# Order of head scores and softmax steps around the start and the end of a decode layer

## The chip, the cores and the metric

One core of a Trainium2 chip runs the kernel. The metric is the time of one execution on the device, in microseconds (us). Times come from repeated runs and from one profiled execution.

## The reference

One token (a row x of 640 values) goes through two layers, each an attention block over a cached window and a small mixer block. The caches K and V, the weights and the order are the same in both layers.

```python
W = 4096                                  # the last 4096 of 32768 cached positions
def A(x):                                 # 32 heads of 192
    q = (x @ wq) by head
    s = einsum("hd,hkd->hk", q, k_cache[:, -W:]) * 192 ** -0.5
    p = softmax(s)
    o = einsum("hk,hkd->hd", p, v_cache[:, -W:])
    return o.reshape(6144) @ wo
def B(x):                                 # one position: the shifted path adds nothing
    x1 = x + 0
    return x1 + gelu(ln(x1) @ w3) @ w4    # 640 -> 1536 -> 640
x = x + A(ln(x)); x = x + B(ln(x))
x = x + A(ln(x)); x = x + B(ln(x))
```

All inputs are bf16. A head's window of K, or of V, is 4096 x 192 values, 1.57 MB. Both layers read nearly all of K and V from memory: 217 MB in all.

## The kernel before, in words

**Loads and cells.** SP issues all loads, in one fixed order (`stream`). K, V and wo go into 11 cells of on-chip memory of 1.57 MB each. `take` hands out the cell that was given back first in program order, and `give` returns one; a load waits on SP until the last use of its cell is over, and everything behind it in the stream waits with it. The wq weights stay resident. The two mixer weights take a cell each at the end of the first layer and keep it.

**Scores.** A head's K is transposed by DVE in four quarters (line 308), which frees the K cell. PE multiplies each quarter with the block form of q (line 358, 48 matmuls a head, 12 a quarter); the result goes to `ST_ps`. In the code `T(h, half)` does two quarters of the transpose and `S(h, half, ...)` the scores of two quarters.

**Kept heads.** In layer 1 (`layer == 0` in the code) the transposed K of heads 0 to 6 (`NKEEP = 7`) stays in seven cells. Layer 2 scores these heads without loading or transposing K again; the cell of a kept head is given back after its second half of scores (`give(("T", h))`). So at the start of layer 2, two cells are taken by mixer weights, seven by kept heads, and two are left for loads. The stream begins layer 2 with V of heads 0, 1, 2, K of head 7, V of head 3 (half of it; the other half waits in PSUM and is copied back by DVE behind the P*V of head 2, line 434), wo of group 0, then K8, V4, K9, V5, K10, V6, K11, V7.

**Groups.** Heads go in eight groups of four: in layer 1 from the last group to the first, in layer 2 from the first to the last. While group g's softmax and P*V run, the scores of group g + 1 are made. The steps of a softmax (`softmax_steps`) are part_max (DVE, line 369), turn_max (PE, line 375), full_max (DVE, lines 380 and 382), spread_max (PE, line 388, then ACT's copy and four exponentials, line 394), swap (PE, line 403, ACT, line 406, PE, line 408) and recip (DVE). The steps of a group's q projection (`qproj_steps`) are project (PE, line 325, 30 matmuls), spread (DVE, line 332), repeat (PE, line 339) and block (DVE, line 344). P*V of a head is `pv` (PE, line 445, 32 matmuls), followed by DVE's transpose into `o_sb` (line 449); `o_fold` is one small product on PE and a scaling on ACT (lines 457 and 458). `out_proj` (line 468) multiplies a group's output with its part of wo. Small products share two PSUM buffers (`psm`).

**The order is written by hand.** Each engine runs its instructions in the order of the program. Before the loop, group 0 is scored, with the first half of its q projection ahead of head 0 and the second half, and `softmax_scale` (1/std of the input; two products on PE and two steps on ACT), ahead of the second head. In the loop, the steps of the softmax are spread between the first two heads of the next group, the other two are scored behind the first two P*V. For the next to last group (`hurry`) both remaining heads are scored behind the second P*V, and the softmax of the last group follows at once: four steps there, the rest behind the third P*V. In layer 2's first pass heads 4 and 5 are scored ahead of the swap, head 6 behind the first P*V, head 7 behind the second.

Of the kernel before, what the change touches and what calls it, by code (L numbers as in the profile page):

```python
# [33 lines left out]
def kernel(  # L34
# [15 lines left out]
    _, _, D = A_x.shape  # L50
    _, H, Sk, Dh = A_k_cache.shape
# [9 lines left out]
    QH = 4  # L61
# [10 lines left out]
    NKEEP, NCELL = 7, 11  # L72
# [240 lines left out]
    def qproj_steps(c, xc, part=None):  # L313

        held = {}
        n = QT if part is None else QT // 2
        t0 = c * QT + (part or 0) * n

        def project():
            need("wq", 0, ND - 1)  # L320
            qT_ps = psm.tile([P, n], F32, tag="psm")
            for tl in range(n):
                t = t0 + tl
                for kc in range(ND):
                    nc.tensor.matmul(  # L325
                        qT_ps[:, tl:tl + 1], lhsT=wq_sb[:, kc, t * P:(t + 1) * P], rhs=xc[:, kc:kc + 1],
                        start=(kc == 0), stop=(kc == ND - 1))
            held["q"] = qT_ps

        def spread():  # L330
            Xq = sm.tile([P, n, 4], BF16, name="Xq")
            nc.vector.tensor_tensor(  # L332
                out=Xq[:], in0=held["q"][:, :].unsqueeze(2).broadcast_to([P, n, 4]),
                in1=maskq[:, :].unsqueeze(1).broadcast_to([P, n, 4]), op=ALU.mult)
            held["x"] = Xq

        def repeat():
            Qrep_ps = psm.tile([P, 4 * n], F32, tag="psm")
            nc.tensor.matmul(Qrep_ps[:], lhsT=Lb[:], rhs=held["x"][:].rearrange("p t b -> p (t b)"),  # L339
                             start=True, stop=True)  # L340
            held["r"] = Qrep_ps

        def block():
            nc.vector.tensor_tensor(
                out=Qblk[:, 4 * t0:4 * (t0 + n), :],
                in0=held["r"][:, :].unsqueeze(2).broadcast_to([P, 4 * n, NM]),
                in1=blkm[:, :].unsqueeze(1).broadcast_to([P, 4 * n, NM]), op=ALU.mult)

        return project, spread, repeat, block
# [125 lines left out]
    def attention(layer, x_cur, rs_cur, x_new, rs_new):  # L475
        groups = GROUPS[layer]
        xc, _, total = ln_center(x_cur, rs_cur)
        y = [x_cur]
        Th = {}
        last_plain = [h for g in groups for h in g if h >= NKEEP][-1]  # L480

        sc = sm.tile([P, 1], F32, name="sc")

        def softmax_scale():
            rstd = power(total(), 1.0, eps1, "rstd")
            nc.vector.tensor_scalar(out=sc[:], in0=rstd[:], scalar1=scale, scalar2=None, op0=ALU.mult)

        def T(h, half):
            for q in (2 * half, 2 * half + 1):
                if (h, q) not in Th:  # L490
                    Th[h, q] = transpose_quart(layer, h, q)

        def S(h, half, ST_ps, hq):
            for q in (2 * half, 2 * half + 1):
                scores_quart(h, Th.pop((h, q)), q, ST_ps, hq)
            if half == 1 and layer == 1 and h < NKEEP:
                give(("T", h))
            if half == 1 and layer == 0 and h == last_plain:
                give(("area", layer))
                area[0] = None  # L500

        def q_now(gi, part=None):
            for step in qproj_steps(groups[gi][0] // QH, xc, part):
                step()

        def add_y(y_ps, last):
            if last:
                nc.vector.scalar_tensor_tensor(out=x_new[:], in0=y_ps[:], scalar=1.0, in1=y[0][:],
                                               op0=ALU.mult, op1=ALU.add, accum_out=rs_new[:, 0:1])
                return  # L510
            y_new = sm.tile([P, ND], F32, name="y_acc")
            nc.vector.tensor_add(y_new[:], y[0][:], y_ps[:])  # L512
            y[0] = y_new

        q_now(0, 0)
        ST = psS.tile([P, 4, NGK, NM], F32, name="ST_ps")
        for hq, h in enumerate(groups[0]):
            if hq == 1:
                q_now(0, 1)
                softmax_scale()  # L520
            for half in range(2):
                if layer == 0:
                    T(h, half)
                else:
                    Th.update({(h, q): transpose_quart(layer, h, q) for q in (2 * half, 2 * half + 1)})
                S(h, half, ST, hq)
        pending = None
        early = None
        for gi, cur in enumerate(groups):
            nxt = list(enumerate(groups[gi + 1])) if gi + 1 < len(groups) else []  # L530
            ST_n = None
            if nxt:
                part_max, turn_max, full_max, spread_max, swap, recip = softmax_steps(len(cur), ST, sc)
                ST_n = psS.tile([P, 4, NGK, NM], F32, name="ST_ps")
                if gi == 0:
                    q_now(1)
                h0 = nxt[0][1]
                T(h0, 0)
                part_max()
                T(h0, 1)  # L540
                S(h0, 0, ST_n, 0)
                turn_max()
                full_max()
                S(h0, 1, ST_n, 0)
                spread_max()
                h1 = nxt[1][1]
                q = None
                if gi + 2 < len(groups):
                    q = qproj_steps(groups[gi + 2][0] // QH, xc)
                if layer == 1 and gi == 0:  # L550

                    for half in range(2):
                        T(h1, half)
                        S(h1, half, ST_n, 1)
                    nxt.pop(1)
                    PT = swap()
                    rl = recip()
                    for step in q:
                        step()
                else:  # L560
                    if q:
                        q[0]()
                    if pending is not None:
                        y_ps = out_proj(layer, *pending)
                    T(h1, 0)
                    if q:
                        q[1]()
                        q[2]()
                    if pending is not None:
                        add_y(y_ps, False)  # L570
                        pending = None
                    PT = swap()
                    T(h1, 1)
                    if q:
                        q[3]()
                    rl = recip()
                nxt.pop(0)
            else:
                if layer == 0:
                    add_y(out_proj(layer, *pending), False)  # L580
                PT, rl = early
            oT = sm.tile([P, NA], BF16, name="oT")
            hurry = gi + 2 == len(groups)
            final = gi + 1 == len(groups)
            fold = None
            for hq, h in enumerate(cur):
                o_sb = pv(layer, h, hq, PT, fold)
                if final:
                    fold = None
                    if hq < QH - 2:  # L590
                        o_fold(h, o_sb, oT, rl)
                    else:
                        def fold(h=h, o_sb=o_sb):
                            o_fold(h, o_sb, oT, rl)

                    continue
                for _ in range(2 if hurry and hq == 1 else 1):
                    if nxt:
                        q2, h2 = nxt.pop(0)
                        for half in range(2):  # L600
                            T(h2, half)
                            S(h2, half, ST_n, q2)
                if hurry and hq == 1:
                    steps = softmax_steps(len(cur), ST_n, sc)
                    steps[0]()
                o_fold(h, o_sb, oT, rl)
                if hurry and hq == 1:
                    for step in steps[1:4]:
                        step()
                if hurry and hq == 2:  # L610
                    early = steps[4](), steps[5]()
            if final:
                if layer == 1:
                    add_y(out_proj(layer, *pending), False)
                fold()
            pending = (cur[0] // QH, oT)
            ST = ST_n
        add_y(out_proj(layer, *pending), True)
# [92 lines left out]
```

## Time and profile before

| | |
|---|---|
| median of 5 runs | 543.34 us (542.81 to 543.76) |
| the profiled execution | 544.75 us, span of the profile 542.9 us |
| PE busy with matmuls | 283.7 us (52%) |
| DVE busy | 257.5 us (47%) |
| ACT busy | 54.6 us (10%) |
| read from memory | 217.06 MB, 400 GB/s over the span |
| granted TensorE clock | 1.00 |

In the profile, busy times are sums over an engine's instructions; a line of waits names who waited for whom; a timeline has start, length, engine, line and form of merged instructions, and in brackets the idle time ahead of them with what ended it ("issue": nothing that the profile shows). Windows give busy times in a stretch of the span, with the mean busy share of the 16 DMA engines and the rate. All times on these views are from the start of the span. The first layer's attention ends near 289 us, its mixer near 296 us, where layer 2 begins.

### The profile page before, as it was taken

To read this page: it belongs to the slowest core of one execution; us is meant where nothing else is said; L and a number is where in the kernel's file an instruction comes from. 1 tells how busy PE (TensorE), PEld (TensorE's weight loads), DVE (VectorE), ACT (ScalarE), POOL (GpSimd) and SP (SyncE) were. 2 spreads that over 40 slices of the span, in tenths; PEclk is the share of its full clock that TensorE was granted. 3 is DMA by queue.
4 is the path that set the end of the run, shared out by engine and by line. 5 is a ranking of instruction groups with operands and counts; after the bars stand their busy time and mean duration, and the time that the engine had idled before them with its cause. 6 is when DMAs were issued, how large, how long until landed. Compare 5 with 4: busy or idle time off the path is not lost.

```text
span 542.9 us, 14848 instructions
## 1 busy us (share of the span) xinstructions
PE 283.7 (52%) x6820; PEld 229.5 (42%) x6820; DVE 257.5 (47%) x494; ACT 54.6 (10%) x249; POOL 2.0 (0%) x11
## 2 busy tenths in 40 slices
PE   0156546365364545545635777656454554636645
PEld 0045435254353434434415755545343443524434
DVE  2187536455554636537212137655463653555511
ACT  1001010010100101010201011010010101001101
POOL 1000000000000000000000000000000000000000
DMA  8999999999999999999999899999999999999980
GB/s 353 426 424 422 421 423 422 422 422 420 424 419 422 425 422 420 425 425 416 370 409 384 310 356 420 423 424 417 426 419 422 421 421 424 421 423 422 423 356 13
DMA packets 23633, 218.00 MB, mean 402 GB/s; under 512 B 2452, under 2 KB 3988, under 8 KB 8084
## 3 DMA queue, kind: packets, MB, share of 16 engines
q1 hardware_dynamic: 23572, 217.07, 96.3%
q8 instruction: 53, 0.87, 0.6%
q14 instruction: 8, 0.07, 0.0%
HBM read 217.06 MB, written 0.00 MB: 400 GB/s over the span
## 4 chain that ended last, share of the span: by engine, by line
DMA 74%; PE 13%; DVE 9%; issue 2%; ACT 1%; SPq 0%; ACTq 0%; DVEq 0%
DMA cell<-in_A_k_cache_dram 54%; DMA cell<-in_A_v_cache_dram 15%; DVE cell L308 7%; PE O_ps L445 4%; PE ST_ps L358 3%; DMA cell<-in_A_wo_dram 3%; DMA wq_sb<-in_A_wq_dram 3%; PE l_ps L408 1%; PE y_ps L468 1%; PE qT_ps L325 1%; PE y_ps L660 1%; PE hT_ps L628 1%; PE PT_ps L403 1%; PE nb_ps L388 0%; ACT PT L406 0%
## 5 line engine op out<-in xcount | busy, mean ns | idle before, releaser
L308 DVE STREAM_TRANSPOSE cell<-cell 128x768 uint32<-128x768 uint32 x228 | 204.4, 946 | 91.9 <-DMA cell<-in_A_k_cache_dram 91.9
L358 PE MATMUL ST_ps<-Qblk,cell 128*128 128x4 bf16 x3072 | 113.8, 168 | 155.4 <-DVE cell L308 153.9
L358 PEld LDWEIGHTS <-cell 128*128 128x128 bf16 x3072 | 97.7, 105 | 187.4 <-DVE cell L308 180.8
L445 PE MATMUL O_ps<-cell,PT 128*1 128x192 bf16 x2048 | 98.3, 359 | 17.1 <-DMA cell<-in_A_v_cache_dram 16.2
L449 DVE STREAM_TRANSPOSE o_sb<-O_ps 128x192 f32<-128x192 f32 x64 | 24.5, 382 | 119.9 <-PE O_ps L445 119.9
L445 PEld LDWEIGHTS <-PT 128*1 128x1 bf16 x2048 | 68.2, 115 | 23.8 <-issue 12.3
L458 ACT ACTIVATE oT<-oT_ps,rl 32x6 bf16<-32x6 f32 x64 | 16.5, 257 | 284.2 <-PE oT_ps L457 284.2
L394 ACT ACTIVATE Pr<-ST_ps,nb_sb,sc 128x32 bf16<-128x32 f32 x64 | 25.1, 488 | 0.5
L325 PE MATMUL qT_ps<-xc,wq_sb 128*128 128x1 bf16 x480 | 16.3, 166 | 15.8 <-DMA wq_sb<-in_A_wq_dram 12.6
L457 PE MATMUL oT_ps<-o_sb,Lq 128*32 128x6 f32 x128 | 17.0, 205 | 12.2 <-DVE o_sb L449 12.1
L325 PEld LDWEIGHTS <-wq_sb 128*128 128x128 bf16 x480 | 15.3, 105 | 16.7 <-DMA wq_sb<-in_A_wq_dram 13.3
L457 PEld LDWEIGHTS oT_ps<-o_sb,Lq 128*32 128x32 f32 x128 | 12.0, 142 | 21.2 <-issue 14.1
L339 PE MATMUL Qrep_ps<-Xq,Lb 128*128 128x24 bf16 (+1 forms) x18 | 3.2, 179 | 28.6 <-DVE Xq L332 28.6
L468 PE MATMUL y_ps<-oT,cell 128*128 128x1 bf16 x480 | 15.3, 166 | 2.9 <-DMA cell<-in_A_wo_dram 1.9
L403 PEld LDWEIGHTS <-Eq 128*32 128x32 bf16 x256 | 4.0, 106 | 29.8 <-DVE y_acc L512 27.4
L468 PEld LDWEIGHTS <-cell 128*128 128x128 bf16 x480 | 14.4, 104 | 3.4 <-DMA cell<-in_A_wo_dram 2.6
L332 DVE TENSOR_TENSOR Xq<-qT_ps,maskq 128x24 bf16<-128x24 f32 (+1 forms) x18 | 2.8, 156 | 26.0 <-PE qT_ps L325 26.0
L390 ACT COPY nb_sb<-nb_ps 128x4 f32<-128x4 f32 x16 | 2.6, 162 | 120.6 <-PE nb_ps L388 120.6
L394 ACT ACTIVATION_READ_ACCUMULATOR Pr<-ST_ps,nb_sb,sc 128x1 f32 x64 | 14.4, 224 | 0.0
L408 PE MATMUL l_ps<-lpart,ones 128*128 128x4 f32 x32 | 9.4, 364 | 5.7 <-ACT PT L406 5.3
L408 PEld LDWEIGHTS l_ps<-lpart,ones 128*128 128x128 f32 x32 | 8.0, 311 | 7.4 <-ACT PT L406 6.7
L388 PE MATMUL nb_ps<-dg,ones 4*128 4x4 f32 x32 | 8.9, 346 | 2.8 <-DVE dg L382 1.7
(85 smaller groups left out, 107.1 us busy)
## 6 DMA issues: line engine op xcount, KB each, us to landing
cell<-in_A_v_cache_dram SPq DMA_DIRECT2D x59, 1536.0 KB, 24.1
cell<-in_A_k_cache_dram SPq DMA_DIRECT2D x57, 1536.0 KB, 26.0
cell<-in_A_wo_dram SPq DMA_DIRECT2D x14, 960.0 KB, 21.6
wq_sb<-in_A_wq_dram SPq DMA_DIRECT2D x5, 1536.0 KB, 12.4
cell<-in_A_v_cache_dram SPq DMA_DIRECT2D x9, 768.0 KB, 19.3
cell<-in_A_wo_dram SPq DMA_DIRECT2D x4, 480.0 KB, 16.0
cell<-in_B_w_dram SPq DMA_DIRECT2D x1, 1536.0 KB, 13.0
cell<-in_B_w_dram SPq DMA_DIRECT2D x1, 1440.0 KB, 14.2
```

The costliest lines, as they stand in the source:

```text
L308: nc.vector.transpose(Tu, Ku[:, :, q * NY:(q + 1) * NY])
L325: nc.tensor.matmul(qT_ps[:, tl:tl + 1], lhsT=wq_sb[:, kc, t * P:(t + 1) * P], rhs=xc[:, kc:kc + 1], start=(kc == 0), stop=(kc == ND - 1))
L358: nc.tensor.matmul(ST_ps[:, hq, q * ng + g, :], lhsT=T4[:, g, f, :, t], rhs=Qblk[:, h * NCOL + 2 * f + t, :], start=(n == 0), stop=(n == N ...
L388: nc.tensor.matmul(nb_ps[:], lhsT=ones[0:n, :], rhs=held["dg"][0:n, :], start=True, stop=True)
L394: nc.scalar.activation(out=Pr[:, hq].rearrange("p m g -> p g m"), in_=ST_ps[:, hq], func=ACTF.Exp, bias=nb_sb[:, hq:hq + 1], scale=sc[:, 0 ...
L403: nc.tensor.matmul(PT_ps[32 * m:32 * (m + 1), :, j, :], lhsT=Eq[:, j, :], rhs=held["Pr"][:, :, m, :], start=True, stop=True)
L408: nc.tensor.matmul(l_ps[:], lhsT=ones[:], rhs=held["l"][:], start=True, stop=True)
L445: nc.tensor.matmul(O_ps[r:r + 1, :], lhsT=PT[:, hq, i:i + 1], rhs=V[:, i * Dh:(i + 1) * Dh], start=(i < 4), stop=(i >= NB - 4))
L449: nc.vector.transpose(o_sb[:], O_ps[:].rearrange("p (a c) -> p c a", c=NA))
L457: nc.tensor.matmul(oT_ps[r, :], lhsT=Lq[:], rhs=o_sb[:, :, 0], start=True, stop=True)
L458: nc.scalar.activation(oT[r, :], oT_ps[r, :], ACTF.Copy, scale=rl[r, 0:1])
L468: nc.tensor.matmul(y_ps[:, n:n + 1], lhsT=wo_t[:, k * D + n * P:k * D + (n + 1) * P], rhs=oT[:, k:k + 1], start=(i == 0 if split else k == 0),
```

## The change

Three orders change; the instructions stay the same.

1. Before the loop, the products of both halves of group 0's q projection come first; the second half's repeat and block come within head 0's scores; `softmax_scale` comes behind the second head. In layer 2, group 1's q projection moves from ahead of the loop into group 0's heads: two steps ahead of the third head, two ahead of the fourth.
2. In layer 2's first pass the kept heads of group 1 (4, 5, 6) are scored in a row with the first steps of the softmax between them. Group 2's projection, the swap and recip follow. Head 7 then comes behind the first P*V.
3. In the next to last group, the last head's second half of scores moves behind the third P*V, with part_max and turn_max; full_max follows the fold; spread_max, swap and recip move behind the fourth P*V.

```diff
-        q_now(0, 0)
+        qa, qb = (qproj_steps(groups[0][0] // QH, xc, part) for part in (0, 1))
+        qa[0]()
+        qb[0]()
+        for step in qa[1:]:
+            step()
+        qb[1]()
         ST = psS.tile([P, 4, NGK, NM], F32, name="ST_ps")
+        q1 = iter(qproj_steps(groups[1][0] // QH, xc))
         for hq, h in enumerate(groups[0]):
-            if hq == 1:
-                q_now(0, 1)
-                softmax_scale()
+            if layer == 1 and hq >= 2:
+                next(q1)()
+                next(q1)()
             for half in range(2):
...
                 S(h, half, ST, hq)
+                if (hq, half) == (0, 0):
+                    qb[2]()
+                    qb[3]()
+            if hq == 1:
+                softmax_scale()
...
                 if layer == 1 and gi == 0:
-                    for half in range(2):
-                        T(h1, half)
-                        S(h1, half, ST_n, 1)
-                    nxt.pop(1)
+                    keep = [hh for hh in nxt if hh[1] < NKEEP]
+                    del nxt[:len(keep)]
+                    q = qproj_steps(groups[2][0] // QH, xc)
+                    part_max()
+                    for i, (q2, h2) in enumerate(keep):
+                        for half in range(2):
+                            T(h2, half)
+                            S(h2, half, ST_n, q2)
+                        if i == 0:
+                            turn_max()
+                            full_max()
+                        if i == 1:
+                            spread_max()
+                    q[0]()
                     PT = swap()
+                    q[1]()
                     rl = recip()
-                    for step in q:
-                        step()
+                    q[2]()
+                    q[3]()
                 else:
+                    if gi == 0:
+                        for step in q1:
+                            step()
...
-                for _ in range(2 if hurry and hq == 1 else 1):
-                    if nxt:
-                        q2, h2 = nxt.pop(0)
-                        for half in range(2):
-                            T(h2, half)
-                            S(h2, half, ST_n, q2)
                 if hurry and hq == 1:
+                    (q2, h2), (q3, h3) = nxt
+                    for half in range(2):
+                        T(h2, half)
+                        S(h2, half, ST_n, q2)
+                    T(h3, 0)
+                    S(h3, 0, ST_n, q3)
+                    T(h3, 1)
+                elif hurry and hq == 2:
+                    S(h3, 1, ST_n, q3)
                     steps = softmax_steps(len(cur), ST_n, sc)
                     steps[0]()
+                    steps[1]()
+                elif nxt and not (hurry and hq == 3):
+                    q2, h2 = nxt.pop(0)
+                    for half in range(2):
+                        T(h2, half)
+                        S(h2, half, ST_n, q2)
                 o_fold(h, o_sb, oT, rl)
-                if hurry and hq == 1:
-                    for step in steps[1:4]:
-                        step()
                 if hurry and hq == 2:
+                    steps[2]()
+                if hurry and hq == 3:
+                    steps[3]()
                     early = steps[4](), steps[5]()
```

More of the change, by code (lines that the diff above doesn't have):

```diff
@@ L500, in S @@
                 area[0] = None
-        def q_now(gi, part=None):
-            for step in qproj_steps(groups[gi][0] // QH, xc, part):
-                step()
         def add_y(y_ps, last):
@@ L534, in attention @@
                 ST_n = psS.tile([P, 4, NGK, NM], F32, name="ST_ps")
[L535 to L549, printed above, removed]
-                if layer == 1 and gi == 0:
-                    for half in range(2):
-                        T(h1, half)
-                        S(h1, half, ST_n, 1)
-                    nxt.pop(1)
+                if layer == 1 and gi == 0:
+                    keep = [hh for hh in nxt if hh[1] < NKEEP]
[12 more added lines that the diff above has]
+                    q[0]()
                     PT = swap()
+                    q[1]()
                     rl = recip()
-                    for step in q:
-                        step()
-                else:
+                    q[2]()
+                    q[3]()
+                else:
+                    if gi == 0:
+                        for step in q1:
+                            step()
+                    h0 = nxt[0][1]
+                    T(h0, 0)
+                    part_max()
+                    T(h0, 1)
+                    S(h0, 0, ST_n, 0)
+                    turn_max()
+                    full_max()
+                    S(h0, 1, ST_n, 0)
+                    spread_max()
+                    h1 = nxt[1][1]
+                    q = None
+                    if gi + 2 < len(groups):
+                        q = qproj_steps(groups[gi + 2][0] // QH, xc)
                     if q:
@@ L576, in attention @@
                     rl = recip()
-                nxt.pop(0)
+                    nxt.pop(0)
             else:
@@ L596, in attention @@
                     continue
-                for _ in range(2 if hurry and hq == 1 else 1):
-                    if nxt:
-                        q2, h2 = nxt.pop(0)
-                        for half in range(2):
-                            T(h2, half)
-                            S(h2, half, ST_n, q2)
-                if hurry and hq == 1:
+                if hurry and hq == 1:
+                    (q2, h2), (q3, h3) = nxt
[7 more added lines that the diff above has]
+                    S(h3, 1, ST_n, q3)
                     steps = softmax_steps(len(cur), ST_n, sc)
                     steps[0]()
+                    steps[1]()
[4 more added lines that the diff above has]
+                        S(h2, half, ST_n, q2)
                 o_fold(h, o_sb, oT, rl)
-                if hurry and hq == 1:
-                    for step in steps[1:4]:
-                        step()
                 if hurry and hq == 2:
+                    steps[2]()
+                if hurry and hq == 3:
+                    steps[3]()
                     early = steps[4](), steps[5]()
```

## The prediction

> **What bounds the kernel now.** I read the chain of waits first, then the rate by slices, then stretches of the boundary between the layers, then the queues of SP and PE there. From the page:
>
> ```profile
> DMA 74%; PE 13%; DVE 9%; issue 2%; ACT 1%; SPq 0%; ACTq 0%; DVEq 0%
> GB/s 353 426 424 422 421 423 422 422 422 420 424 419 422 425 422 420 425 425 416 370 409 384 310 356 420 423 424 417 426 419 422 421 421 424 421 423 422 423 356 13
> ```
>
> The loads bound the kernel: 422 GB/s nearly throughout, while PE is 52% busy and DVE 47%. An instruction moved elsewhere is worth nothing. What can be won is in slices 19 to 23 (258 to 326 us) and in the tail after the last load. The same stretch in windows (us, busy time of PE, PEld, DVE, ACT, POOL, clock, DMA share, GB/s):
>
> ```profile
> 297.00:302.00 5.00, 3.92 (x114) 3.61 (x114) 1.10 (x7) 0.77 (x4) 0.00 (x0) 1.00 0.54 173
> 302.00:310.50 8.50, 5.43 (x187) 5.18 (x185) 0.78 (x5) 0.00 (x0) 0.00 (x0) 1.00 0.99 413
> 310.50:322.00 11.50, 8.82 (x232) 7.41 (x228) 2.59 (x10) 2.26 (x11) 0.00 (x0) 1.00 0.85 316
> 322.00:326.00 4.00, 2.54 (x69) 2.28 (x73) 2.84 (x4) 0.26 (x1) 0.00 (x0) 1.00 0.98 382
> 360.00:500.00 140.00, 74.49 (x1816) 60.90 (x1816) 72.18 (x128) 14.36 (x67) 0.00 (x0) 1.00 1.01 422
> ```
>
> Against 422 GB/s the first window loses 5 x (422 - 173) / 422 = 2.95 us, the third 11.5 x 106 / 422 = 2.89, the fourth 4 x 40 / 422 = 0.38. Why: SP's timeline (start, length, queue and line of the load).
>
> ```profile
> 286.50 13.86 SPq L129 DMA_DIRECT2D cell<-in_A_v_cache_dram  x3
> 302.63 0.33 SPq L117 DMA_DIRECT2D cell<-in_A_k_cache_dram  x1
> 305.19 0.33 SPq L129 DMA_DIRECT2D cell<-in_A_v_cache_dram  x1
> 311.01 0.33 SPq L142 DMA_DIRECT2D cell<-in_A_wo_dram  x1
> 313.09 0.33 SPq L117 DMA_DIRECT2D cell<-in_A_k_cache_dram  x1
> 317.50 0.33 SPq L129 DMA_DIRECT2D cell<-in_A_v_cache_dram  x1
> 318.86 0.42 SPq L117 DMA_DIRECT2D cell<-in_A_k_cache_dram  x1
> ```
>
> By the order of the stream these are V0 to V2 (V2 at 300.0, the row's end), K7, the half of V3, wo0, K8, V4, K9. Each waits for a cell. Data flow about 2.0 us after an issue: V2 at 300.0, the rate is back at 302.0. A whole K or V (1.57 MB) takes 3.73 us at 422, wo0 2.33, the half 1.86. PE in the same stretch:
>
> ```profile
> 297.32 0.54 PE L325 MATMUL qT_ps<-xc,wq_sb 128*128 128x1 bf16 x15 [0.26 <-DVE xc L263]
> 298.58 1.42 PE L358 MATMUL ST_ps<-Qblk,cell 128*128 128x4 bf16 x48 [0.30 <-DVE Qblk L344]
> 301.18 3.98 PE L358 MATMUL ST_ps<-Qblk,cell 128*128 128x4 bf16 x144
> 305.02 0.83 PE L325 MATMUL qT_ps<-xc,wq_sb 128*128 128x1 bf16 x26
> 308.30 0.25 PE L325 MATMUL qT_ps<-xc,wq_sb 128*128 128x1 bf16 x4 [2.45 <-issue]
> 311.62 1.44 PE L358 MATMUL ST_ps<-Qblk,cell 128*128 128x4 bf16 x48
> 317.39 1.44 PE L358 MATMUL ST_ps<-Qblk,cell 128*128 128x4 bf16 x48
> 320.32 0.65 PE L445 MATMUL O_ps<-cell,PT 128*1 128x192 bf16 x12 [0.47 <-issue]
> ```
>
> Heads 0 to 3 are scored by 300.0, 302.5, 303.8 and 305.2, head 4 by 311.0, head 5 by 313.1; head 6 only by 318.8, behind the first P*V. SP's times follow one for one: wo0 has head 4's cell, K8 head 5's, V4 the cell of V0 (P*V ended 317.4), K9 head 6's. PE itself pauses 2.45 us with nothing to wait for, at "issue". A code load of 16 KB begins at 305.7 as it pauses (53 such packets in the instruction queue); 256 instructions are 128 matmuls, 3.4 us here. Counting PE's instructions in the trace in blocks of 256 back from this pause, the time from entering one block to having the next was 6.0 us (302.3 to 308.3) and 5.6 (314.8 to 320.3, the last row's pause).
>
> **The change part by part.** I work on the clock of this execution: 544.75 us with a span of 542.9, 1.41 above the median of 543.34. The saving is subtracted from the median.
>
> *Start of layer 2, V2.* The second projection comes first: 15 more matmuls on PE (15 x 0.031 = 0.47), of which the 0.26 spent waiting for Xq is cover. The repeat starts 0.16 later; the second repeat inside head 0 costs 0.03. Head 0's cell comes free at 300.2, not 300.0. V2 and everything behind it: +0.2.
>
> *Heads 1 to 3.* Head 1 follows at once, but its last matmuls lie in the next code block, which was entered at 302.28 before and can hardly be there sooner: its load began 299.6 and ended 300.7, and 1.5 us more passed at the other pause. So head 1 ends about 302.2 (K7 no later than before). Then 0.5 of softmax_scale, 0.9 of group 1's projection, head 2, and 43 matmuls of head 3, to 306.1. There the count of instructions is that of the old pause. With 6.0 us from 302.1 PE waits until 308.1 and head 3 ends 308.3, 3.1 later than before. It frees V3's half: its data come at 310.3, where K7 ends at 309.8 or so. New gap: 0.5.
>
> *Heads 4 to 6 in a row.* The projection is gone from here. Head 4 by 309.6 (wo0, 1.4 sooner), turn_max, head 5 by 311.0 (K8, 2.1 sooner), 0.5 for the spread of the maxima, then head 6, whose middle lies in the next code block (there at 308.1 + 6.0 = 314.1): it ends at 314.8. V4 now takes head 6's cell: issued 314.8 against 317.50, data at 316.8. The transfers by then: V3's half ends 312.2, wo0 314.5, K8 318.2. All three gaps close, and V4 runs without one.
>
> *P*V of head 0, then head 7.* Projection 0.8, swap 0.3, copy 0.3, l 0.5, P*V 1.4: ends 318.3. K9 gets this cell: data at 320.3, wanted at 321.9, slack 1.6. Head 7 now comes ahead of P*V of head 1: its four transposes (3.52 us) run from 318.7 to 322.3 on DVE, behind nothing but o_sb; V5 takes K7's cell: data at 324.3, wanted at 325.6, slack 1.3. P*V of head 1, the fold and V3's restore stand behind it on PE and DVE, but K10, V6 and K11 have over 3 us each. The first softmax runs beside the scoring: its exponentials end near 313.4 (0.2 and 1.6 after the maxima are spread at 311.5), the swap starts at 315.6.
>
> *Sum.* Recovered 2.89 + 0.38 = 3.27; given back 0.2 + 0.5. That is 2.6 us. It lasts, since from 326 on the queue is ahead and stays so (422).
>
> *Code loading from both sides.* No row shows it in the new order. Not below 5.6 us: head 3 is 0.4 sooner and the gap nearly gone, gain 3.0. The longest such step in the trace is 7.6 (288.4 to 296.0): head 3 ends 309.9, the gap before V3's half is 2.1, V4's 0.1; gain 0.9. I take 6.0, the row in this very stage. The Trainium skill ("Runtime: NRT & Kernel Launch", Instruction fetch mechanics) holds instruction loading to be mostly hidden by the pace of the sequencer; the 2.45 us row says otherwise here, and by the rule alone head 3 would end near 306.3 and the sum be 3.1.
>
> *Start of layer 1.* The same steps, but PE waits 3.8 us for the first K's transposes there, and the loads are at 422. Nothing.
>
> *The last softmax, both layers.* The work is the same; it moves behind the third P*V, its end behind the fourth. DVE's transposes that free K cells keep their places, and no load waits longer: P*V of the third head no longer stands behind half a head's scores, a turn and a spread (262.7 to about 260.2), so V1's and V2's cells come sooner. In layer 1 the next group's first P*V needs the new softmax at about 269.1 against 268.7, and the second waited 1.47 us for V. In layer 2, V27 is there at 512.8, so P*V of head 28 starts near 518.4 instead of 516.57; the waits for loads behind it are 1.49, 0.85, 1.08, 1.01 and 1.55 us. Cost 0; without that cover, 1.9. The tail after the last wo is untouched.
>
> **The rivals.** *Code loading sets the pace.* For it: two pauses in 15 us already. Each block 1.6 us later leaves 0.9: 542.4. *The lost rate is not on the transfer path that ends last.* The 16 engines drift apart by several us; whichever is behind idles less in a gap, so the mean overstates. Against it, the last share of V3's half landed at 311.6 and that of V4 at 326.3: 14.7 us for 9.8 us of bytes (wo0, K8, V4). A gain of some 0.6: 542.7. *Slower: the first P*V starves the queue.* K9 hangs on P*V of head 0 and V5 on head 7, now queued before the second P*V. Beyond 1.3 us of lateness each costs one for one; the gain is gone at 3.9. Two more pauses of 2.45 beyond those counted make 4.9, three 7.4: 543.34 + 7.4 - 3.9 = 546.8. Against it, blocks are 6 us apart and PE waits on DVE there anyway.
>
> **How the numbers follow.** Forecast 543.34 - 2.6 = 540.7, chance 0.68, own range 539.9 (nearly all recovered, restarts cheaper) to 541.6. Code loading 0.13, drift 0.10, starving 0.09. What a measurement can tell is about 0.2%, 1.1 us: faster takes the forecast and two thirds of code loading, 0.77; drift and the rest 0.14; slower 0.09. A range of 539.6 to 542.6 leaves out the starving, half the drift and the lower fringe, under 0.2.
>
> **What would show it.** Right: wo0, K8 and V4 issue near 309.6, 311.0 and 314.8 with x2 at the same time, no second and third gap, V3's half later than 307, an "issue" pause inside head 3's scores. Wrong: V4 issued after 317, a gap at K9 or V5, or PE late for the last wo.

## The result and the profile after

The changed kernel takes 542.19 us (median of 20 runs, 541.49 to 542.96), the kernel before 543.53 (39 runs, 542.18 to 545.12). The ratio is 0.9973, 95% interval 0.9967 to 0.998: 1.3 to 1.5 us faster, where 2.6 were forecast. The profiled execution took 542.02 us with a span of 540.2; that of before took 544.75 with 542.9. The two profiles differ by 2.7 us, and half of that is not in the medians.

The chain of waits and the rate by slices of the changed kernel:

```profile
GB/s 352 428 423 422 418 425 424 422 423 419 423 421 425 422 422 421 422 424 422 409 402 376 297 394 422 421 421 423 425 419 422 422 420 424 421 422 423 422 371 26
DMA 72%; PE 15%; DVE 10%; issue 1%; ACT 1%; SPq 0%; DVEq 0%; ACTq 0%
```

The loads bound it as before; slices 19 to 23 (counted from 0) are still the only dent ahead of the tail. The windows of that stretch (us, busy time of PE, PEld, DVE, ACT, POOL, clock, DMA share, GB/s):

```profile
297.00:302.00 5.00, 4.11 (x131) 3.92 (x132) 0.90 (x6) 0.30 (x2) 0.00 (x0) 1.00 0.42 124
302.00:310.50 8.50, 6.51 (x227) 6.37 (x226) 1.44 (x6) 0.46 (x2) 0.00 (x0) 1.00 0.99 394
310.50:322.00 11.50, 8.25 (x212) 7.08 (x213) 4.59 (x10) 2.26 (x11) 0.00 (x0) 1.00 0.97 386
322.00:326.00 4.00, 2.65 (x54) 1.54 (x43) 1.78 (x4) 0.51 (x2) 0.00 (x0) 1.00 1.02 428
```

The third window went from 316 to 386 GB/s and the fourth from 382 to 428, but the second fell from 413 to 394 and the first from 173 to 124. SP's queue says when each load was issued, in the order V0 to V2, K7, V3's half, wo0, K8, V4, K9:

```profile
286.85 13.60 SPq L129 DMA_DIRECT2D cell<-in_A_v_cache_dram  x3
301.88 0.33 SPq L117 DMA_DIRECT2D cell<-in_A_k_cache_dram  x1
307.82 0.33 SPq L129 DMA_DIRECT2D cell<-in_A_v_cache_dram  x1
309.10 0.33 SPq L142 DMA_DIRECT2D cell<-in_A_wo_dram  x1
310.59 0.80 SPq L117 DMA_DIRECT2D cell<-in_A_k_cache_dram  x1
313.13 0.33 SPq L129 DMA_DIRECT2D cell<-in_A_v_cache_dram  x1
316.62 0.33 SPq L117 DMA_DIRECT2D cell<-in_A_k_cache_dram  x1
```

wo0 came 1.9 us sooner than before, K8 2.5 and V4 4.4; V3's half came 2.6 later, V2 at 300.1 as before. The forecast had 308.3, 309.6, 311.0 and 314.8 for the four loads from V3's half to V4; they came 0.4 to 1.7 sooner. PE shows the reason for V3's half:

```profile
297.37 0.94 PE L325 MATMUL qT_ps<-xc,wq_sb 128*128 128x1 bf16 x30 [0.26 <-DVE xc L263]
299.31 1.98 PE L358 MATMUL ST_ps<-Qblk,cell 128*128 128x4 bf16 x69
301.62 0.22 PE L358 MATMUL ST_ps<-Qblk,cell 128*128 128x4 bf16 x3 [0.34 <-issue]
304.24 1.31 PE L358 MATMUL ST_ps<-Qblk,cell 128*128 128x4 bf16 x44
307.55 1.53 PE L358 MATMUL ST_ps<-Qblk,cell 128*128 128x4 bf16 x52 [1.99 <-issue]
312.32 0.78 PE L358 MATMUL ST_ps<-Qblk,cell 128*128 128x4 bf16 x23 [0.48 <-issue]
```

The three blocks of code end where they were counted to end: in the last matmuls of head 1 (a pause of 0.34), in head 3 (1.99) and in head 6 (0.48). From 301.6, where PE enters a block, to 307.55, where it has the next, are 5.9 us. The block after that was there sooner, at 312.32 or 4.8 us later, and so was V4, which waits for head 6. The moved softmax at the end of layer 2, P*V of head 28, the first three matmuls of head 29's (the other 29 follow at 517.64) and the second half of head 30's:

```profile
515.58 1.45 PE L445 MATMUL O_ps<-cell,PT 128*1 128x192 bf16 x32
517.57 0.33 PE L445 MATMUL O_ps<-cell,PT 128*1 128x192 bf16 x3
521.34 0.81 PE L445 MATMUL O_ps<-cell,PT 128*1 128x192 bf16 x16 [0.83 <-DMA cell<-in_A_v_cache_dram]
```

The first of them starts at 515.58, the 518.4 of the forecast less the 2.7 by which the whole end is earlier, and the waits for V return with the last row (0.83 us). Whether any of it reaches the end is asked of e3 below.

### The profile page after: what moved, and what is told of

Same layout as the page of the kernel before. It is cut to its first block, busy times and chain, and to the rows that moved or that the text cites. A ratio compares the mean times of both kernels' runs of the same rounds, so it can differ in the third digit from the quotient of the medians.

```text
span 540.2 us, 14848 instructions
## 1 busy us (share of the span) xinstructions
PE 282.0 (52%) x6820; PEld 229.2 (42%) x6820; DVE 257.6 (48%) x494; ACT 54.6 (10%) x249; POOL 2.0 (0%) x11
## 4 chain that ended last, share of the span: by engine, by line
DMA 72%; PE 15%; DVE 10%; issue 1%; ACT 1%; SPq 0%; DVEq 0%; ACTq 0%
DMA cell<-in_A_k_cache_dram 57%; DMA cell<-in_A_v_cache_dram 10%; DVE cell L308 8%; PE O_ps L445 5%; PE ST_ps L358 3%; DMA cell<-in_A_wo_dram 3%; DMA wq_sb<-in_A_wq_dram 3%; PE l_ps L408 1%; PE y_ps L468 1%; PE y_ps L688 1%; PE hT_ps L656 1%; PE qT_ps L325 1%; PE PT_ps L403 1%; DVE o_sb L449 0%; PE nb_ps L388 0%
```

## The experiments

The theory: the change gains what the loads V3's half, wo0, K8 and V4 gain by being issued sooner, and the rest of the forecast was lost because V3's half came too late, into a queue that had run dry. The rivals: the last softmax costs what is missing; the first profile of before was a bad execution; or the small loads are slow in themselves. Each ratio is to the kernel before, timed on the same chip.

**The parts of the change, one at a time.** e1 has only the first part of the diff (projections and `softmax_scale`), e2 only the row of kept heads, e3 only the last softmax (lines shortened and run together):

```diff
 e1: +        qa[0]()                # and the rest of part 1
     +            if layer == 1 and hq >= 2: next(q1)(); next(q1)()
 e2: +                    for i, (q2, h2) in enumerate(keep): ...   # q_now(1) stays ahead of it
 e3: +                elif hurry and hq == 2: S(h3, 1, ST_n, q3); ...
```

> Only the first part: both projections of group 0 ahead, softmax_scale behind the second head, group 1's projection inside group 0's heads; the kept heads and the last softmax as before. Theory (gaps): head 3 ends near 308 as in the changed kernel, head 4 near 309.2 without a projection ahead of it, head 5 near 310.6, and P*V of head 0, which frees V4's cell, near 316 instead of 317.5; the second gap closes and most of the third. Nearly the whole gain of the full change, 1.0 to 1.5 us in the medians. Rival (the last softmax eats half): more than the full change gains, 2.4 to 2.8 us.

Measured: 541.96 us against 543.59, ratio 0.9973 (0.9962 to 0.9984): as much as the full change gains. The queue of SP in it, V3's half, wo0, K8 and V4:

```profile
308.19 0.33 SPq L129 DMA_DIRECT2D cell<-in_A_v_cache_dram  x1
309.69 0.33 SPq L142 DMA_DIRECT2D cell<-in_A_wo_dram  x1
311.77 0.33 SPq L117 DMA_DIRECT2D cell<-in_A_k_cache_dram  x1
316.18 0.33 SPq L129 DMA_DIRECT2D cell<-in_A_v_cache_dram  x1
```

K8 and V4 come 1.2 and 3.1 us later than in the full change, and it does not show in the time. With wo0 and K8 still being moved, V4 at 316.2 is not late: the rate from 318 to 322 is 436 GB/s. From 302 to 326 e1 runs at 388 GB/s, the full change at 396; the difference is worth 0.5 us, which these medians can't tell. The forecast gave the third gap to the row of heads; the first part alone closes nearly all of it (379 GB/s from 310.5 to 322, against 316 before and 386 in the full change).

> Only the row of kept heads 4, 5, 6 with group 2's projection behind it; group 1's projection stays ahead of the row, so head 4 still ends near 311 and wo0 is no sooner: the second gap stays, the third (V4, now on head 6's cell near 314.5) goes. Theory (gaps): 0.4 to 1.0 us faster in the medians. Rival (the last softmax eats half): 1.2 to 1.6.

Measured: 542.81 us, ratio 0.9989 (0.9979 to 1.0). About 0.6 us, at the edge of what can be told. V4 came at 314.2, as expected of the row, and wo0 at 310.2, 0.4 to 0.8 us sooner than in the two profiles of before; from 302 to 326 the rate was 381 GB/s. So the row alone raises the rate too (356 and 361 before), but what e1 and e2 gain in rate does not add up in the full change (396).

> Only the move of the last softmax behind the third and fourth P*V of the group before, in both layers. Theory (gaps): the wait is covered, within 0.3 us of before. Rival (the last softmax eats half): 1.0 to 1.4 us slower, with P*V of the last group's heads late for their loads.

Measured: 543.72 us, ratio 0.9998 (0.999 to 1.0006). The last softmax neither costs nor gains more than about half a microsecond; that rival falls.

**The kernel before again (e4).**

> The kernel before, unchanged: a second profiled execution of it. Theory (gaps, the first profiled execution being 1.2 us above the median of all runs): the loss between 302 and 326 us is smaller than the 3.4 us of the first profile, near 2. Rival (the last softmax eats half): the same 3.4 us and a span near 542.9 again.

Measured: 543.75 us over 11 runs, the profiled execution 543.93, span 542.2. Its windows from 310.5 to 326:

```profile
310.50:322.00 11.50, 8.37 (x215) 6.99 (x213) 2.35 (x9) 2.25 (x11) 0.00 (x0) 1.00 0.89 306
322.00:326.00 4.00, 2.72 (x73) 2.46 (x77) 2.67 (x4) 0.26 (x1) 0.00 (x0) 1.00 0.97 400
```

From 302 to 326 the rate was 356 GB/s, 361 in the first profile: a loss of 3.5 to 3.8 us, no smaller. So the first profile was not unlucky there, against my expectation. It differs at the start: PE paused 0.69 us ("issue") at the end of the mixer, where its code packet began at 293.6; here the packet began at 292.5, there was no pause, and V2 was issued at 299.3 instead of 300.0. The forecast used that step only as a bound on a block's length (288.4 to 296.0). Between the profiles at the medians (543.93 and 542.02) lie 1.9 us, not 2.7.

**The new gap at V3's half (e5, e6).** In layer 2 the working cell of DVE's transposes is taken in program order ahead of V3's half, so it gets head 2's cell and V3 head 3's, although it is wanted only near 317. One line in `transpose_quart` turns this round; in e6 it also hands wo0, K8 and V4 a cell one head sooner:

```diff
             if area[0] is None:
+                if layer == 1:
+                    need("v", 1, VKEEP)          # e5;   VKEEP + 1 in e6
                 area[0] = take(("area", layer))
```

> The changed kernel, with the working cell of layer 2's transposes taken behind V3's half in program order: V3's half gets head 2's cell (free near 304.2) and the working cell is head 3's (308). Nothing else moves. Theory (the new gap is an empty queue: V3's half is issued as the queue runs dry, and loads issued one by one into a dry queue reach full rate only after about 3.5 us): V3's half issues near 304.3, the stretch from 309 to 313.5 goes from about 285 GB/s to 380 or more, 0.6 to 1.2 us faster than the changed kernel. Rival (these small transfers are slow in themselves): the stretch stays near 300 GB/s and the time as the changed kernel's.

Measured: 541.49 us, ratio 0.9964 (0.995 to 0.9977), against 541.99 and 0.9974 for the changed kernel timed together with it (e8): 0.5 us, just under the 0.6 expected. V3's half was issued at 304.35 and the stretch from 309 to 313.5 rose to 357 GB/s, less than expected:

```profile
309.00:313.50 4.50, 3.47 (x103) 3.29 (x100) 0.56 (x2) 1.74 (x9) 0.00 (x0) 1.00 1.00 357
```

wo0 came no sooner (309.6), head 6 now paused 1.03 us for code, and V4 came at 314.2, so from 302 to 326 the rate was 393 GB/s and had not risen. The profiled execution, 541.81 us, was the slowest of the seven.

> As the one before, but the working cell is taken behind V4: V3's half, wo0, K8 and V4 each get the cell of one head earlier (heads 2, 3, 4, 5), the working cell is head 6's (313, wanted near 317). Theory (empty queue): wo0 issues near 308, K8 near 309.3, V4 near 310.8, and the whole stretch from 309 to 322 runs at 400 GB/s or more; 1.0 to 1.4 us faster than the changed kernel, 2.5 us or more faster than before. Rival (small transfers are slow in themselves): no more than 0.3 us faster than the changed kernel.

Measured: 541.4 us, ratio 0.9962 (0.9947 to 0.9977): 0.6 us below the changed kernel, less than the 1.0 expected. The intervals of the two ratios overlap, but five of the six runs lie below all but one of the twelve of e8. The two loads, V3's half and wo0, in e6, and the stretch from 309 to 313.5 us, first of the changed kernel, then of e6:

```profile
304.53 0.33 SPq L129 DMA_DIRECT2D cell<-in_A_v_cache_dram  x1
307.97 0.33 SPq L142 DMA_DIRECT2D cell<-in_A_wo_dram  x1
```

```profile
309.00:313.50 4.50, 4.02 (x123) 3.84 (x120) 0.56 (x2) 1.74 (x9) 0.00 (x0) 1.00 0.90 286
```

```profile
309.00:313.50 4.50, 2.99 (x85) 2.81 (x82) 0.56 (x2) 1.74 (x9) 0.00 (x0) 1.00 1.02 418
```

The same loads in the same order, issued 1.1 to 3.3 us sooner, keep the rate at 418 GB/s instead of 286. So these loads are not slow in themselves; here they were slow when each was issued as the one ahead of it ran out. In the changed kernel that stretch loses 4.5 x (422 - 286) / 422 = 1.45 us, where the forecast had a gap of 0.5. But a pause of PE grew with the fuller queue. Head 3's and head 6's in e6:

```profile
307.70 1.52 PE L360 MATMUL ST_ps<-Qblk,cell 128*128 128x4 bf16 x52 [2.00 <-issue]
313.84 0.77 PE L360 MATMUL ST_ps<-Qblk,cell 128*128 128x4 bf16 x23 [1.85 <-issue]
```

Head 3's pause is as in the changed kernel. Head 6 pauses 1.85 us, 0.48 in the changed kernel and not at all in e8. The packet with its code began 3.6 us after PE entered the block ahead (311.3 against 307.7); in the changed kernel, beside the half-empty queue, 2.0 us (309.5 against 307.55), and 1.05 in e8.

**Where the code blocks end (e7, e8, e11, e10).** 64 matmuls with an unused result, in layer 1 where PE waits 6 us for V, move all later blocks by 128 instructions:

```diff
+                if final and layer == 0 and hq == 3:
+                    for _ in range(64):
+                        nc.tensor.matmul(pad_ps[:], lhsT=Lb[:], rhs=Lb[:, 0:1], start=True, stop=True)
                 o_sb = pv(layer, h, hq, PT, fold)
```

> The changed kernel with 64 extra matmuls (128 PE instructions, result unused) in layer 1 ahead of the last P*V, where PE waits 6 us for a load. Theory (PE's pauses are code loads in blocks of 256 instructions): the pauses in layer 2 move 64 matmuls earlier: one of about 2 us inside head 2's scores, none inside head 3's, and 54 code packets or the same 53; head 3 ends within 0.5 us of where it did. Rival (the pause belongs to head 3's work, a wait that the profile doesn't show): it stays inside head 3's scores.

Measured: 541.25 us in one run, 54 packets. The pause left head 3, so it does not belong to that head's work. But it did not appear in head 2: PE stood 0.63 us in head 0 and 2.44 in head 5, 64 matmuls ahead of the old place in head 6. The block in head 2 was there in time; its packet had begun at 300.9, in the gap ahead of V2's data. V3's half came at 305.8 and wo0 at 307.1, and the stretch from 309 to 313.5 ran at 413 GB/s.

> The changed kernel again, on the same chip as its variants: near 542.2 us and 1.3 us below before; its second profile should again show a pause of about 2 us in head 3's scores and the stretch from 309 to 313.5 near 285 GB/s.

Measured: 541.99 us over 12 runs, ratio 0.9974 (0.9964 to 0.9984), pause 2.27 us, 288 GB/s. As expected; only head 6 had no pause for code here.

> e7 again, timed: the changed kernel with the 64 unused matmuls. Theory (in the changed kernel a pause of 2 us in head 3 holds V3's half until the queue is dry; elsewhere it does less): 0.5 to 0.9 us faster than the changed kernel, near e6. Rival (e7's single time was chance): as the changed kernel, 541.9 to 542.3.

Measured: 541.06 us, ratio 0.9957 (0.9943 to 0.9971). Faster than the changed kernel by about 0.9 us by the ratios (0.9974 in e8); the intervals overlap.

> e6 with the 64 unused matmuls of e7. Theory (the queue is full in e6, so the place of PE's code pauses no longer matters): the same time as e6 within 0.4 us. Rival (the pauses cost the path themselves): 0.6 us or more faster than e6.

Measured: 540.48 us, ratio 0.9949 (0.9937 to 0.9962): the best of all, 2.7 us below before, and 0.7 below e6 by the ratios, again with overlapping intervals. The time fits the rival better, that the pauses count even with a full queue; with the overlap, and with e12 below, that is not shown. Where the pauses were in its profile, in head 5 and in the swap:

```profile
308.26 1.12 PE L360 MATMUL ST_ps<-Qblk,cell 128*128 128x4 bf16 x36 [1.60 <-issue]
314.43 0.29 PE L405 MATMUL PT_ps<-Pr,Eq 128*32 128x32 bf16 x5 [2.14 <-issue]
```

Neither holds V3's half, wo0 or K8, which were issued at 303.6, 304.9 and 306.2. From 302 to 326 it ran at 421 GB/s.

**The first part with early cells (e9).** e1 and the line of e6, no row, no moved softmax.

> The first part of the change alone, with the cells handed out early as in e6 (working cell behind V4), the kept heads and the last softmax as before. Theory (what counts is when V3's half, wo0, K8 and V4 are issued): V3's half near 304.5, wo0 near 308, K8 near 309.7, V4 near 311.8; 402 GB/s or more from 302 to 326; within 0.3 us of e6, so about 2 us faster than before. Rival (the row of heads is needed): V4 or K9 late, 0.6 us or more behind e6.

Measured: 541.27 us, ratio 0.9965 (0.9952 to 0.9978), 414 GB/s from 302 to 326. Level with e6; the row of heads is not needed.

**The shift without the change (e12).**

> The kernel before, with the 64 unused matmuls in layer 1 and nothing else changed. Theory (the pause for code in group 1's projection held wo0, and the pauses are where the blocks of 256 instructions happen to end): the 2.4 us pause ahead of head 4 goes (the next one falls inside head 5), wo0 issues near 308.2 instead of 311.0, the loss between 302 and 326 us falls from 3.5 to about 1.5, and the kernel is 1.0 to 1.8 us faster than before, as much as the change itself. Rival (what counts is only the order of scores and projection): within 0.4 us of before.

Measured: 544.25 us over 12 runs, ratio 1.001 (0.9995 to 1.0025). By the time the rival holds. By its profile the theory does: wo0 at 308.0, and from 302 to 326:

```profile
302.00:326.00 24.00, 17.93 (x486) 15.31 (x484) 7.68 (x20) 2.78 (x13) 0.00 (x0) 1.00 1.00 415
```

But that execution took 541.09 us and was the shortest; three of the twelve lie at 541.1 to 541.8, nine at 543.7 to 545.2. What the longer ones do was not seen, as the kernel has one profile. The other shifted kernels are split too: three of e11's six runs lie at 539.9 to 540.6 and three at 541.5 to 541.9. The shift alone is no gain in the median. Whether the code of the longer executions came later, or something else did, stays open, and so does the share of the code blocks in e10's 0.7 and e11's 0.9.

All profiles together: the rate over the whole boundary, the landing of the last share of the last wo (a load lands in 16 shares, one for each DMA engine), the time of this same execution, and the ratio of the medians:

| kernel | GB/s, 258 to 326 us | last share lands, us | this execution, us | ratio |
|---|---|---|---|---|
| before (first, e4) | 365, 366 | 532.5, 531.7 | 544.75, 543.93 | 1 |
| e3 last softmax only | 365 | 530.9 | 543.15 | 0.9998 |
| e2 row only | 372 | 531.0 | 543.24 | 0.9989 |
| e1 first part only | 373 | 530.3 | 542.47 | 0.9973 |
| the change (first, e8) | 376, 376 | 529.8, 529.7 | 542.02, 541.91 | 0.9973, 0.9974 |
| e5 | 377 | 529.6 | 541.81 | 0.9964 |
| e7 | 379 | 529.0 | 541.25 | one run |
| e6 | 380 | 529.3 | 541.53 | 0.9962 |
| e9 | 384 | 528.8 | 541.03 | 0.9965 |
| e12 | 385 | 528.8 | 541.09 | 1.001 |
| e11 | 386 | 528.2 | 540.36 | 0.9957 |
| e10 | 387 | 527.8 | 539.99 | 0.9949 |

Execution by execution the time falls as the rate rises, e12 included; apart from the three profiles at 365 and 366, neighbours are out of order by 0.3 us at most. e12's median doesn't fit, since most of its runs were unlike the profiled one. From 365 to 376 GB/s over 68 us is 68 x 11 / 422 = 1.8 us, and the medians moved 1.3 to 1.5. The three profiles at 365 and 366 end up to 1.6 us apart, so a single profile can't settle the last half microsecond.

## Why the prediction was right, and where its sum was off

*The place and the mechanism* held: cells that come free sooner, loads issued sooner, second and third gap smaller, the gain kept to the end. *The last softmax* held (e3). *The start of layer 1* was put at nothing; e1 has it and shows no loss, but no run has it alone.

*The size* was not right. 542.19 us lies above the forecast's own range, 539.9 to 541.6, and inside the wide one, which was stretched over the rival of code loading. That rival's 542.4 is close by luck: its condition, every block 1.6 us later, did not occur.

*The code blocks* held in place, with pauses in heads 1, 3 and 6, and for one step in length: 5.9 us against the 6.0 taken. The next took 4.8, below the forecast's bound ("Not below 5.6 us"; the row under that bound, 314.8 to 320.3, is 5.5), and in e8 head 6 did not wait. That is why V4 came 1.7 us sooner than forecast.

*The term that was off is the new gap before V3's half.* The sum gave back 0.5 for it and let wo0 and K8 follow without a break ("All three gaps close"). The step behind it took 2.0 us from an issue to the flow of data, read at V2, and a full rate from then on. With V3's half at 307.82, wo0 at 309.10 and K8 at 310.59 the rate from 309 to 313.5 was 286 GB/s: 1.45 us. So from 302 to 326 the loss fell from 24 x 61 / 422 = 3.5 us to 24 x 26 / 422 = 1.5, by 2.0 instead of the 2.6 to 2.8 that the terms of that stretch come to. In e6 and e7 both V3's half and wo0 are issued sooner, and the same stretch runs at 418 and 413 GB/s; in e5, with V3's half alone, at 357. The late issue of these two was the cause.

*The give-back at V2* was 0.2 in the sum. The first window lost 5 x 49 / 422 = 0.6 more than before, while the 39 us ahead of it ran at 397 instead of 392 GB/s and won 0.5: the loads ended sooner and waited longer for the same V2. Against the first profile that is close to the term; against e4, with V2 at 299.3, the same working gives 0.6.

*The starting point* was one execution, 1.2 us above the later median. It makes the two profiles differ by 2.7 us, but it is not why the sum was off: e4, 0.2 above its own median, lost as much from 302 to 326. From e4 to the changed kernel the profiled executions differ by 1.9 us and the medians by 1.3 to 1.5; that half microsecond stays open.

*The row of heads* was given the third gap. e1 closes nearly all of it without the row. With two changes that free the same load, the later issue of V4 did no harm that the times show once wo0 and K8 had moved up.

*The other rivals* fall. Drift (the mean rate overstates, a gain of 0.6): the last share lands 1.9 us sooner than in e4, no less than the 1.6 that the mean rates of the two give. The forecast had argued against it from a wrong reading: the last share of V3's half landed at 313.3, not 311.6, so it was 13.0 us, not 14.7, for 9.8 us of bytes. Starving: K9 was issued at 316.6, 2.2 us sooner than before, and the rate from 322 to 326 was 428 GB/s.

The Trainium skill ("Runtime: NRT & Kernel Launch", Instruction fetch mechanics) holds instruction loading mostly hidden. The pauses of 1.99 and 2.27 us in the two profiles of the changed kernel say that on this dense stretch of PE it is not; they moved with the count of instructions in e7.

## What to carry to other kernels

When loads bound a kernel, cost a moved instruction by the load that it lets go, and check every load behind it for the queue's depth at that time: a load issued as the queue runs dry costs more than its own gap. Look at which buffer each request is handed in program order: giving a buffer that is wanted late to the request that comes first held a load here by 3.5 us, and one line that also moved the three loads behind it gave 0.6. Take a second profile of the kernel before, ahead of subtracting microseconds from one.

## What was unexpected

Code packets of PE came later the fuller the queue of loads was. For the block that PE enters in head 6, the packet began 1.05 and 2.0 us after PE entered the block ahead in the two profiles of the changed kernel, where the queue was running dry, 3.1 us after in e5 and 3.6 in e6, where it was full; in the gap ahead of V2's data (e7) it was 1.1. The pause in head 6 went from none and 0.48 to 1.03 and 1.85 us. That the packets wait behind the loads is a reading of these profiles; no run tests it alone. And 64 unused matmuls went with a shorter time in two kernels (0.9957 and 0.9949, against 0.9974 and 0.9962 without, on another chip and with overlapping intervals) but not in a third (1.001).
